# Routing slots by token blocks, one narrowing step fewer in four experts, and a third buffer for f

## The chip, the cores and the metric

The kernel runs on one core of one Trainium2 chip. The metric is the device time of the whole program in microseconds (us); it is given as the median of several runs.

## What is computed

Three parts follow one another. First a linear attention with a decay for each key dimension, over 4 batches, 8 heads, 768 steps and 48 dimensions a head; its output is taken as 3072 tokens of 384 numbers. Then a mixture of eight experts in which every token has one expert and every expert exactly 384 tokens, dealt out greedily by the logits. Last a gated network behind an RMS norm. Cut to what matters:

```python
f = 1 / (1 + exp(-f_logit))                       # attention, for every batch and head
for t in range(768):
    state = f[t][:, None] * state + outer(k[t], v[t])
    y[t] = q[t] @ state
x = y as [3072, 384]
logits = x @ w_gate                               # experts: 8, capacity 384
for idx in argsort(-logits.flatten()):            # best pair of token and expert first
    give the token to the expert if the token is free and the expert not full
out[mask_e] = relu(x[mask_e] @ w1[e]) @ w2[e]
xn = out / rms(out) * rms_g                       # last network, width 1536
result = (silu(xn @ w2_gate) * (xn @ w2_val)) @ w2_out
```

The three weights of the last network come as float64, so the kernel first narrows them to float32 with integer operations.

## The kernel before, in words

**Attention** (`attention`) works on 16 units, each a pair of heads of one batch. A loop over i interleaves the stages of neighbouring units by hand: `scans(i + 1)` on VectorE (two scans over 768 steps, a product with k), `k_back`, `inner`, `sums` and `values` on TensorE, copies on ScalarE, masks and products with q on GpSimd. `decays(i + 2)` on ScalarE turns raw f into decays. `load("kqf", i + 4)` at the end of an iteration (L638) puts the next loads on SyncE's queue, which works in that order. Raw k and raw q have three buffers, raw f has two (`NR`, L363), so the load of f for unit i + 4 goes into the buffer that `decays(i + 2)` has just read. The first load into each buffer takes all 128 rows with their padding; later ones take the 96 rows that change, in two parts (L381, L384).

**Routing** (`Route`) finds eight thresholds in five steps; each step compares on VectorE (`hits`, L75) and counts on TensorE. The last `choose` writes A, a one-hot choice of an expert for every token, with `is_equal` in two halves (L175). A has the layout [128, expert, block], the token's number being 128 times its block (24 of them) plus its partition, so this write goes with a stride. `slots` (L294) then gives every token its place within its expert: a scan on VectorE (`cum`, L309) adds up A along the blocks for each expert, TensorE multiplies with a triangle and with ones and leaves the count of tokens ahead in `pre`; VectorE takes the choice's own (`pos`, L314), adds over the experts (`ps1`, L316), splits the place into a block of 128 and a rest (L318 to L322), multiplies W by the block's flags (L325), compares the rest with 0 to 127 in three calls of `hits`, and 24 matmuls (L334) turn all into the list `idx` of the tokens of each expert. A gather by `idx` then fetches the rows of the first expert.

**Experts**: `expert(e)` runs over eight column blocks j. For each j TensorE makes `h` (9 matmuls of 384 columns; each product is split into high and low parts, hence three matmuls where one would do, L673 to L675), ScalarE writes `hh` (L1146), VectorE the low part `hl` (L1147), and TensorE does `second(e, j - 2)`, 9 matmuls that read `hh` and `hl` of two blocks earlier. `second` for j = 6 and 7 comes behind the loop. `side(e, j)` puts the other work in between:

```python
if j in ((1, 2, 3, 4) if e == 0 else (1, 3, 4, 5) if e < 5 else (1, 3, 5)):
    narrow_step()
if 0 < j < 5:
    piece_split(W1[e + 1, j - 1])        # high and low part of the next expert's weights
...
if j > 4:
    xpose(e + 1, j - 5)                  # transposes of the next expert's rows
...
if j > 5:
    narrow_step()
```

A `narrow_step` is a stage of a small pipeline: it writes back a finished tile (ScalarE's queue), narrows an earlier one (`narrow2`: L1067 on ScalarE, L1068, L1069, L1071 on VectorE, L1072 and L1073 on GpSimd) and loads another (L1058 on SyncE's queue). There are 36 tiles and 40 calls: six in each of the experts 0 to 4, five in experts 5 and 6, none in the last. The order of the instructions on each engine is the order of the program; no planner moves them.

**Last network**: 12 blocks of 256 tokens, bound to the narrowed weights, mostly TensorE.

Of the kernel before, what the change touches and what calls it, by code (L numbers as in the profile page):

```python
# [35 lines left out]

def more_consts(tc, cst, K):
    nc = tc.nc
    edge = K["edge"]
    inc = cst.tile([128, 128], F32, name="inc")  # L40
    K.update(inc=inc, up=cst.tile([128, 128], BF, name="up"))
    nc.gpsimd.tensor_scalar(inc[:, 0:1], edge[:, 0:1], 1.0, 0.0, op0=OP.mult, op1=OP.add)
    nc.gpsimd.tensor_tensor(out=inc[:, 1:], in0=edge[:, 1:], in1=edge[:, :-1], op=OP.subtract)
    ed = cst.tile([128, 128, 4], BF, name="edges")
    nc.gpsimd.tensor_scalar(ed, edge[:, :, None].to_broadcast([128, 128, 4]), 1.0, 0.0, op0=OP.mult, op1=OP.add)
    up0 = cst.tile([128, 128], BF, name="up0")
    nc.gpsimd.memset(up0, -(2.0 ** -7))
    lim = cst.tile([128, 2], F32, name="lim")
    for c, a, b in ((0, 1.0, -1.0), (1, 384.0, -383.5)):
        nc.gpsimd.memset(lim[:, c:c + 1], a)  # L50
        nc.gpsimd.memset(lim[0:1, c:c + 1], b)
    tri = cst.tile([128, 128], BF, name="tri_bf")
    nc.gpsimd.memset(tri, -1.0)
    nc.gpsimd.affine_select(out=tri, in_=tri, pattern=[[-1, 128]], compare_op=OP.is_ge, fill=0.0, base=0,
                            channel_multiplier=1)
    first = cst.tile([128, 8, 24], F32, name="first")
    nc.gpsimd.memset(first, 1.0)
    nc.gpsimd.memset(first[:, :, 0:1], 0.0)
    ids = cst.tile([128, 24], F32, name="ids")
    nc.gpsimd.iota(ids, pattern=[[128, 24]], base=0, channel_multiplier=0, allow_small_or_imprecise_dtypes=True)  # L60
    pid = cst.tile([128, 1], F32, name="pid")
    nc.gpsimd.iota(pid, pattern=[[0, 1]], base=0, channel_multiplier=1, allow_small_or_imprecise_dtypes=True)
    K.update(tri=tri, first=first, ids=ids, pid=pid, ed=ed, up0=up0, lim=lim)

# [16 lines left out]
class Route:  # L81
# [176 lines left out]
    def run(self, n, flag, idx, ident, rows=None, side=None, more=None):  # L258
# [3 lines left out]

        def check(wk, ps, cum):
# [5 lines left out]
            nc.tensor.matmul(ct[:, 0:E], self.K["ones"], cum[:, :, self.NB - 1], start=True, stop=True)  # L269
            nc.tensor.matmul(ct[:, E:], self.K["ones"], bad, start=True, stop=True)  # L270
            if more:
                more()

            def verdict():
                nc.vector.tensor_scalar(c9[:, 0:E], ct[:, 0:E], self.CAP, None, op0=OP.not_equal)
                nc.vector.tensor_scalar(c9[:, E:E + 2], ct[:, E:], 0.0, None, op0=OP.not_equal)
                nc.vector.tensor_reduce(out=flag, in_=c9, axis=AX.X, op=OP.max)

            return verdict

        with self.tc.tile_pool(name="rf_wk", bufs=1) as wk:
# [12 lines left out]
def slots(tc, K, A, ident, idx, check=None):  # L294
# [3 lines left out]
    with tc.tile_pool(name="s_wk", bufs=1) as wk, tc.tile_pool(name="s_ps", bufs=1, space=PSUM) as ps:  # L298
        fl = "p e n -> p (e n)"
# [4 lines left out]
        nc.gpsimd.tensor_tensor(out=W[:, 0, :, 0], in0=A, in1=K["pid"][:, 0:1, None].to_broadcast([128, E, NB]), op=OP.mult)  # L304
        nc.gpsimd.tensor_tensor(out=W[:, 1, :, 0], in0=A, in1=K["ids"][:, None, :].to_broadcast([128, E, NB]), op=OP.mult)
# [7 lines left out]
        pos = wk.tile([128, E, NB], F32, name="pos")  # L313
# [22 lines left out]
        spin(nc, ps.tile([128, 128], F32, name="spin"), ident, 12)  # L336
        nc.vector.tensor_reduce(out=t1[:, :, 0:3], in_=tb.rearrange("p j (e c) -> p e c j", c=3), axis=AX.X, op=OP.add)
# [3 lines left out]

def attention(tc, fT, kT, qT, vL, YT, w_gate, lg, pmin, ident, gcol, rms_g, bank0, extra):

# [18 lines left out]
    one = bank0[:, 0:1]  # L362
    NR = dict(f=2, k=3, q=3)  # L363
    RAW = {(nm, i): cst.tile([128, S], F32, name=f"raw_{nm}{i}") for nm in "fkq" for i in range(NR[nm])}
    NV = 4
# [3 lines left out]
    def raw(nm, i):  # L369
        return RAW[nm, i % NR[nm]]  # L370

    def load(names, i):
        if not 0 <= i < NU:
            return
        for nm in names:
# [3 lines left out]
            src, t = dict(f=fT, k=kT, q=qT)[nm][i], raw(nm, i)  # L379
            if i < NR[nm]:  # L380
                nc.sync.dma_start(t, src)  # L381
                continue
# [8 lines left out]

    mask = cst.tile([128, C], F32, name="mask")
    nc.gpsimd.memset(mask, 1.0)
# [8 lines left out]
    lgp = YP[0][:, 384:432].rearrange("p (n e) -> p n e", e=8)  # L402
    sel = cst.tile([128, 2, 2, 3, 8], F32, name="sel")
    for t in YP:
# [64 lines left out]
    def k_back(i, gs=(0, 1)):  # L469
        if 0 in gs:  # L470
            KN[i] = wk.tile([128, NC, 128], F32, name="kn")
        a, m = (0, NC - 1) if len(gs) == 2 else (3 * gs[0], 3 - gs[0])
# [62 lines left out]
    def logits(b):  # L535

        o = bank()[:, 0:256]
        for k in range(NP):
            for r in range(4):
# [7 lines left out]
                                 start=k == 0, stop=k == NP - 1)  # L547
        LG[b] = wk.tile([128, 256], F32, name="lgT")
        nc.scalar.copy(LG[b], o)
# [23 lines left out]
    for i in range(-1, NU + 2):  # L573
# [59 lines left out]
        if i == NU - 1:  # L633
# [3 lines left out]
            extra["edges"](bank())  # L637
        load("kqf", i + 4)  # L638
        if i == NU + 1:
# [153 lines left out]
def tile_kernel(ctx, tc, q, k, v, f_logit, w_gate, w1, w2, w2_gate, w2_val, w2_out, rms_g, fT, kT, qT, vL, out):  # L793
# [32 lines left out]
    lg = rc.tile([128, NT // 128, E], F32, name="lg")  # L826
    A = rc.tile([128, E, NT // 128], BF, name="A")
    pmin = rc.tile([128, 1], F32, name="pmin")
# [8 lines left out]
    def edges(bank):  # L837
        R[0].start(bank)
        R[0].early(ytp, bank0[:, 8:16])

    def consts(bank):
        K.update(route_consts(tc, rc))
        more_consts(tc, rc, K)

# [4 lines left out]
    ctx.enter_context(tc.manual_schedule())  # L849
    attention(tc, fT, kT, qT, vL, YT, w_gate, lg, pmin, ident, gcol, rms_g, bank0,  # L850
              {-2: consts, 1: lambda bank: turn_inc(tc, K, bank[:, 0:128], ident), "range": prepare,
# [59 lines left out]
    with ExitStack() as st:  # L911
        with tc.tile_pool(name="rw", bufs=9) as rw, tc.tile_pool(name="rwp", bufs=4, space=PSUM) as rwp:
            for i in range(4):
# [25 lines left out]
        with tc.If(rv > 0):  # L939
# [6 lines left out]
            with tc.If(rv2 > 0):  # L946
                slow_attention(tc, q, k, v, f_logit, x_dram, w_gate, lg, lg_dram, ident)
                slow_route(tc, K, lg, A.rearrange("p e n -> p n e"), ident)
                slots(tc, K, A, ident, idx)
# [60 lines left out]
    with ExitStack() as c1:  # L1010
# [310 lines left out]
```

## Time and profile before

| | |
|---|---|
| median of 3 runs | 815.48 us (815.25 to 815.67) |
| the profiled execution's own time | 811.92 us |
| span of the profiled execution | 810.2 us |
| TensorE matmul busy | 786.3 us, 97% |
| VectorE busy | 484.5 us, 60% |
| ScalarE busy | 391.0 us, 48% |
| GpSimd busy | 276.3 us, 34% |

A view by stretches gives, for each stretch of the span, how long each engine was busy. The timeline gives single instructions: start, duration, engine, line, operation, written tile, read tile, shape, and in brackets how long the engine stood idle before it and what ended that. PE is TensorE, PEld its weight load, DVE VectorE, ACT ScalarE, POOL GpSimd, SP SyncE.

### The profile page before, as it was taken

The numbers are of one execution on the slowest core, as the hardware profiler recorded it, in microseconds if no ns is written. First come the engines' busy times: TensorE is split into PE (matmuls) and PEld (weight loads), VectorE is DVE, ScalarE is ACT, GpSimd is POOL, SyncE is SP. The second block draws the span as 40 slices with busy tenths as digits, with TensorE's granted clock in tenths as the row PEclk, the third lists the DMA queues.
The fourth block names the chain that finished last, engine by engine and source line by source line (L and its number), as shares of the span: only waits on it lengthen the run. The fifth ranks groups of instructions, "written<-read, shape, count | busy, mean of one in ns | idle before, by whom it ended". The sixth has DMA issues, their size and how long they took to land.

```text
span 810.2 us, 17022 instructions
## 1 busy us (share of the span) xinstructions
PE 786.3 (97%) x6809; PEld 768.3 (95%) x6809; DVE 484.5 (60%) x854; ACT 391.0 (48%) x853; POOL 276.3 (34%) x332
## 2 busy tenths in 40 slices
PE   8999986999999999999999999999999999999996
PEld 7888875999999899999999999999999999999996
DVE  8999875988988898466344343444443434434331
ACT  5888561564555555665434343434344342424221
POOL 7898603377777776240101111111201011111110
PEclk9999997999999999999999999999999999999999
DMA  8999553787678669231000000000000000000000
GB/s 266 234 235 220 186 180 120 258 305 256 235 259 306 231 244 334 89 113 40 20 1 21 2 20 1 20 2 20 13 8 21 2 20 1 21 1 21 1 20 20
DMA packets 44262, 88.50 MB, mean 109 GB/s; under 512 B 5904, under 2 KB 23568, under 8 KB 44176
## 3 DMA queue, kind: packets, MB, share of 16 engines
q1 hardware_dynamic: 35072, 70.80, 28.1%
q0 software_dynamic: 3104, 9.44, 3.2%
q10 hardware_dynamic: 6000, 7.09, 2.5%
q8 instruction: 55, 0.90, 0.5%
q14 instruction: 31, 0.25, 0.1%
HBM read 70.81 MB, written 16.52 MB: 108 GB/s over the span
## 4 chain that ended last, share of the span: by engine, by line
PE 65%; issue 8%; DVE 7%; DMA 1%; ACT 1%; POOL 1%; POOLq 0%; ACTq 0%; DVEq 0%
PE o L674 5%; PE g L673 5%; PE g L674 5%; PE v L675 5%; PE v L673 5%; PE g L675 5%; PE v L674 5%; PE o L673 5%; PE o L675 5%; PE h L674 3%; PE h L675 3%; PE h L673 3%; PE x L674 3%; PE x L675 2%; PE x L673 2%
## 5 line engine op out<-in xcount | busy, mean ns | idle before, releaser
L1246 DVE TENSOR_TENSOR hf<-sg,v 128x256 f32<-128x256 f32 x144 | 60.0, 416 | 180.4 <-PE v L675 132.1
L1249 ACT CAST hh<-hf 128x256 fp32r<-128x256 f32 x144 | 58.6, 407 | 138.7 <-DVE hf L1246 138.7
L1007 POOL TENSOR_TENSOR xlo<-xn,xhi 128x256 fp32r<-128x256 f32 x36 | 29.5, 823 | 276.1 <-ACT xhi L1006 276.1
L674 PE MATMUL g<-xlo,w 128*128 128x256 f32 x432 | 119.2, 276 | 0.0
L675 PE MATMUL g<-xhi,w 128*128 128x256 f32 x432 | 119.2, 276 | 0.0
L673 PE MATMUL v<-xhi,w 128*128 128x256 f32 x432 | 119.2, 276 | 0.0
L674 PE MATMUL v<-xlo,w 128*128 128x256 f32 x432 | 119.2, 276 | 0.0
L675 PE MATMUL v<-xhi,w 128*128 128x256 f32 x432 | 119.2, 276 | 0.0
L673 PE MATMUL g<-xhi,w 128*128 128x256 f32 x432 | 119.2, 276 | 0.0
L1244 ACT ACTIVATE sg<-g 128x256 f32<-128x256 f32 x144 | 55.4, 384 | 99.4 <-PE g L675 99.0
L1250 DVE TENSOR_TENSOR hl<-hf,hh 128x256 fp32r<-128x256 f32 x144 | 61.3, 425 | 68.1 <-ACT hh L1249 63.3
L674 PE MATMUL o<-w,hh 128*128 128x384 f32 x288 | 97.0, 337 | 0.0
L673 PE MATMUL o<-w,hh 128*128 128x384 f32 x288 | 96.6, 335 | 0.0
L675 PE MATMUL o<-w,hl 128*128 128x384 f32 x288 | 96.2, 334 | 0.0
L673 PEld LDWEIGHTS g<-xhi,w 128*128 128x128 f32 x432 | 81.1, 188 | 0.0
L675 PEld LDWEIGHTS v<-xhi,w 128*128 128x128 f32 x432 | 81.1, 188 | 0.0
L673 PEld LDWEIGHTS v<-xhi,w 128*128 128x128 f32 x432 | 81.1, 188 | 0.0
L674 PEld LDWEIGHTS v<-xlo,w 128*128 128x128 f32 x432 | 81.1, 188 | 0.0
L675 PEld LDWEIGHTS g<-xhi,w 128*128 128x128 f32 x432 | 81.1, 188 | 0.0
L674 PEld LDWEIGHTS g<-xlo,w 128*128 128x128 f32 x432 | 81.0, 188 | 0.0
L870 DVE TENSOR_TENSOR w<-wraw,w 128x1536 fp32r<-128x1536 f32 x35 | 70.7, 2019 | 5.9 <-ACT w L867 5.5
L1072 POOL TENSOR_TENSOR nr<-nr,ne 128x384 f32<-128x384 f32 x36 | 53.1, 1476 | 48.8 <-DVE ne L1071 26.3
(244 smaller groups left out, 1877.4 us busy)
## 6 DMA issues: line engine op xcount, KB each, us to landing
wraw<-in_moe_w_dram SPq DMA_DIRECT2D x32, 768.0 KB, 6.7
v<-in_v_rows_dram SPq DMA_DIRECT2D x16, 288.0 KB, 5.1
x_dram<-xrows SPq DMA_DIRECT2D x24, 192.0 KB, 2.2
nraw<-in_moe_w_gate_dram SPq DMA_DIRECT2D x12, 384.0 KB, 4.2
nraw<-in_moe_w_val_dram SPq DMA_DIRECT2D x12, 384.0 KB, 3.5
nraw<-in_moe_w_out_dram SPq DMA_DIRECT2D x12, 384.0 KB, 3.7
raw_f<-in_f_logit_turned_dram SPq DMA_DIRECT2D x28, 144.0 KB, 4.5
raw_k<-in_k_turned_dram SPq DMA_DIRECT2D x26, 144.0 KB, 5.4
```

Of the source, the lines that this page charges most:

```text
L673: nc.tensor.matmul(out, lhs[0], rhs[0], start=first, stop=False)
L674: nc.tensor.matmul(out, lhs[0], rhs[1], start=False, stop=False)
L675: nc.tensor.matmul(out, lhs[1], rhs[0], start=False, stop=last)
L870: eng.tensor_tensor(out=lo, in0=raw, in1=hi.bitcast(F32), op=OP.subtract)
L1007: eng.tensor_tensor(out=lo, in0=s, in1=hi.bitcast(F32), op=OP.subtract)
L1072: nc.gpsimd.tensor_tensor(out=r, in0=r, in1=e2.bitcast(F32), op=OP.mult)
L1244: nc.scalar.activation(sg, pg, AF.Silu)
L1246: nc.vector.tensor_tensor(out=h, in0=sg, in1=pv, op=OP.mult)
L1249: nc.scalar.copy(hh, h)
L1250: nc.vector.tensor_tensor(out=hl, in0=h, in1=hh.bitcast(F32), op=OP.subtract)
```

## The change

- **A by blocks.** A becomes [128, block, expert]; `choose` writes it without a stride, and everything in `slots` follows that order.
- **Block sums by TensorE.** The scan `cum` and its constant `first` go. Instead two matmuls with A as weights (96 of its columns each) against ones give the sum of each block and expert, laid out with blocks and experts on the partitions; VectorE copies the 96 x 256 result from PSUM to `sums`, and two matmuls of `sums` with a constant `upto` add the blocks up into `pre`. One more matmul stands in `check`. `upto` is made by two GpSimd instructions (`blocks_ahead`) near the end of the attention, from a small constant `of` that VectorE makes at the start.
- **W behind the first comparison.** The two products of W with the flags (old L325) are issued behind the first of the three calls of `hits`.
- **Narrowing.** Expert 0 gets seven steps, experts 1 to 6 five each, the last expert three, of which one narrows a tile and two only write back; 40 in all, as before.
- **Buffers.** Raw f gets three buffers, and the loads of a unit go in the order f, k, q. To make room, `kn` loses its unused last block, `lgT` has one buffer, two small tiles move to another pool, and the pool of `xrows` has 8 buffers in place of 9.

```diff
-    first = cst.tile([128, 8, 24], F32, name="first")
-    nc.gpsimd.memset(first, 1.0)
-    nc.gpsimd.memset(first[:, :, 0:1], 0.0)
+    of = cst.tile([96, 8], F32, name="of")
+    nc.vector.tensor_reduce(out=of, in_=ident[0:96, 0:96].rearrange("k (n e) -> k e n", e=8), axis=AX.X, op=OP.add)
...
+def blocks_ahead(nc, K):
+
+    o = K["upto"]
+    nc.gpsimd.tensor_scalar(o, K["of"][:, None, None, :].to_broadcast([96, 2, 24, 8]), 1.0, 0.0, op0=OP.mult, op1=OP.add)
+    nc.gpsimd.affine_select(out=o, in_=o, pattern=[[-96, 2], [8, 24], [1, 8]], compare_op=OP.is_ge, fill=0.0, base=0,
+                            channel_multiplier=-1)
...
-                m = self.choose(wk, A.rearrange("p e n -> p n e"))
+                m = self.choose(wk, A)
...
-        pre = ps.tile([128, E, NB], F32, name="pre")
+        spare = ps.tile([128, 2, 128], F32, name="spin")
+        for h in range(2):
+            nc.tensor.matmul(spare[0:96, h], A[:, 12 * h:12 * h + 12].rearrange(fl), K["ones"], start=True, stop=True)
+        sums = wk.tile([96, 2, 128], BF, name="sums")
+        nc.vector.tensor_copy(sums, spare[0:96])
+        pre = ps.tile([128, NB, E], F32, name="pre")
         nc.tensor.matmul(pre.rearrange(fl), K["tri"], A.rearrange(fl), start=True, stop=False)
-        cum = wk.tile([128, E, NB], BF, name="cum")
-        nc.vector.tensor_tensor_scan(out=cum.rearrange(fl), data0=K["first"].rearrange(fl), data1=A.rearrange(fl),
-                                     initial=0.0, op0=OP.mult, op1=OP.add)
-        nc.tensor.matmul(pre.rearrange(fl), K["ones"], cum.rearrange(fl), start=False, stop=True)
-        verdict = check(wk, ps, cum) if check else None
+        for h in range(2):
+            nc.tensor.matmul(pre.rearrange(fl), sums[:, h], K["upto"][:, h].rearrange(fl), start=False, stop=h == 1)
+        verdict = check(wk, ps, sums) if check else None
...
-        nc.vector.tensor_reduce(out=ps1, in_=pos.rearrange("p e n -> p n e"), axis=AX.X, op=OP.add)
+        nc.vector.tensor_reduce(out=ps1, in_=pos, axis=AX.X, op=OP.add)
...
-        for c in (1, 2):
-            nc.vector.tensor_tensor(out=W[:, :, :, c], in0=W[:, :, :, 0],
-                                    in1=ge[:, c, None, None, :].to_broadcast([128, 2, E, NB]), op=OP.mult)
...
             hots.update(hits(nc, K["cm"], "ro", K["io"], r, g, 8))
+            for c in (1, 2) if g == 0 else ():
+                nc.vector.tensor_tensor(out=W[:, :, :, c], in0=W[:, :, :, 0],
+                                        in1=ge[:, c, None, None, :].to_broadcast([128, 2, E, NB]), op=OP.mult)
...
-    NR = dict(f=2, k=3, q=3)
+    NR = 3
...
-        load("kqf", i + 4)
+        load("fkq", i + 4)
...
-        with tc.tile_pool(name="rw", bufs=9) as rw, tc.tile_pool(name="rwp", bufs=4, space=PSUM) as rwp:
+        with tc.tile_pool(name="rw", bufs=8) as rw, tc.tile_pool(name="rwp", bufs=4, space=PSUM) as rwp:
...
-                if j in ((1, 2, 3, 4) if e == 0 else (1, 3, 4, 5) if e < 5 else (1, 3, 5)):
+                if j in ((1, 2, 3, 4, 5) if e == 0 else (1, 3, 5)):
                     narrow_step()
...
+                if j in (0, 1, 3):
+                    narrow_step()
                 if j:
                     piece_split(W2[j - 1])
```

## Rows read from the trace of the kernel before

**Rows 1.** Stretches by stage: length, busy us of each engine, granted clock, DMA.

```profile
0.00:104.00 104.00, 100.48 (x1821) 88.90 (x1822) 95.24 (x125) 75.17 (x220) 81.46 (x143) 0.98 0.85 222
104.00:138.00 34.00, 25.27 (x269) 22.23 (x268) 25.31 (x88) 15.11 (x28) 4.62 (x7) 0.85 0.45 158
138.00:357.00 219.00, 214.06 (x1254) 210.96 (x1254) 180.92 (x243) 122.31 (x193) 141.01 (x102) 1.00 0.72 246
357.00:810.00 453.00, 446.52 (x3473) 446.20 (x3471) 183.05 (x401) 178.41 (x413) 49.21 (x81) 1.00 0.04 13
```

**Rows 2.** Waits of TensorE in the experts, 145 to 350 us: total, times, longest.

```profile
PE x L674 <- DVE hl L1147: 4.3, 4, 1.2
```

**Rows 3.** Stretches of 8 us at the ends of experts 4 and 5, same columns.

```profile
269.50:277.50 8.00, 6.59 (x38) 5.95 (x37) 7.68 (x15) 2.73 (x6) 5.34 (x6) 1.00 0.66 224
296.00:304.00 8.00, 8.00 (x50) 7.92 (x49) 7.32 (x13) 3.11 (x7) 4.42 (x5) 1.00 0.69 233
```

**Rows 4.** Timeline of VectorE late in experts 4 and 5, and hl of expert 0.

```profile
164.34 0.55 DVE L1147 SCALAR_TENSOR_TENSOR hl<-h,hh 128x384 fp32r<-128x384 f32 x1
...
270.06 0.71 DVE L1068 TENSOR_SCALAR nb<-nraw 128x384 int32<-128x384 int32 x1
...
272.45 0.55 DVE L1036 TENSOR_TENSOR xlo<-xT,xhi 128x384 fp32r<-128x384 f32 x1
...
275.96 0.55 DVE L1147 SCALAR_TENSOR_TENSOR hl<-h,hh 128x384 fp32r<-128x384 f32 x1
...
295.87 0.70 DVE L1068 TENSOR_SCALAR nb<-nraw 128x384 int32<-128x384 int32 x1
...
297.55 0.55 DVE L1036 TENSOR_TENSOR xlo<-xT,xhi 128x384 fp32r<-128x384 f32 x1
...
301.06 0.55 DVE L1147 SCALAR_TENSOR_TENSOR hl<-h,hh 128x384 fp32r<-128x384 f32 x1
```

**Rows 5.** Timeline of TensorE at the last `second` of experts 0, 4 and 5.

```profile
165.90 0.34 PE L674 MATMUL x<-hl,w 128*128 128x384 f32 x1
...
275.04 0.34 PE L673 MATMUL x<-hh,w 128*128 128x384 f32 x1
276.56 0.44 PE L674 MATMUL x<-hl,w 128*128 128x384 f32 x1 [1.18 <-DVE hl L1147]
...
303.04 0.34 PE L674 MATMUL x<-hl,w 128*128 128x384 f32 x1
```

**Rows 6.** Two lines of the narrowing: ns of one, least, median and most.

```profile
L1069 DVE SCALAR_TENSOR_TENSOR nb<-nraw,nb x36: 557/560/1264, 154.0 to 322.8; 128x384 int32<-128x384 int32 x36
...
L1072 POOL TENSOR_TENSOR nr<-nr,ne x36: 1003/1020/2417, 155.1 to 324.0; 128x384 f32<-128x384 f32 x36
```

**Rows 7.** Timeline of VectorE around the last choice and the slots.

```profile
120.24 0.42 DVE L175 TENSOR_TENSOR oh<-open,m 128x96 bf16<-128x96 f32 x2
...
124.00 0.42 DVE L170 SCALAR_TENSOR_TENSOR open<-T,down 128x96 f32<-128x96 f32 x2 [0.33 <-PE T L242]
124.34 0.40 DVE L173 TENSOR_REDUCE m<-open 128x12 f32<-128x96 f32 x2
124.66 1.02 DVE L175 TENSOR_TENSOR A<-open,m 128x96 bf16<-128x96 f32 x2
...
126.68 0.36 DVE L314 TENSOR_TENSOR pos<-pre,A 128x192 f32<-128x192 f32 x1
127.07 0.62 DVE L316 TENSOR_REDUCE ps<-pos 128x24 f32<-128x192 f32 x1
```

**Rows 8.** Timeline of TensorE in the slots.

```profile
129.53 2.28 PE L334 MATMUL tb<-W,cm 128*128 128x48 bf16 x24 [2.63 <-DVE cm L75]
```

**Rows 9.** Timeline of ScalarE and VectorE at the fourth unit of the attention.

```profile
20.61 0.86 ACT L424 ACTIVATE G<-raw_f 128x768 f32<-128x768 f32 x1 [0.21 <-DMA raw_f<-in_f_logit_turned_dram]
...
21.79 1.75 DVE L450 TENSOR_TENSOR_SCAN P<-G,bank 128x768 f32<-128x768 f32 x1 [0.70 <-ACT fs L427]
```

More of the change, by code (lines that the diff above doesn't have):

```diff
@@ L34, in route_consts, with more_consts @@
     return dict(io=io, ones=ones, edge=bits.bitcast(F32))
-def more_consts(tc, cst, K):
+def more_consts(tc, cst, K, ident):
     nc = tc.nc
@@ L62, in more_consts @@
     nc.gpsimd.iota(pid, pattern=[[0, 1]], base=0, channel_multiplier=1, allow_small_or_imprecise_dtypes=True)
-    K.update(tri=tri, first=first, ids=ids, pid=pid, ed=ed, up0=up0, lim=lim)
+    K.update(tri=tri, of=of, upto=cst.tile([96, 2, 24, 8], BF, name="upto"), ids=ids, pid=pid, ed=ed, up0=up0, lim=lim)
+def blocks_ahead(nc, K):
[3 more added lines that the diff above has]
+                            channel_multiplier=-1)
 def turn_inc(tc, K, bank, ident):
@@ L261, in run, with check @@
         nc, E, A = self.tc.nc, self.E, self.A
-        def check(wk, ps, cum):
+        def check(wk, ps, sums):
             c9, bad = self.c9, self.bad
@@ L268, in check @@
             ct = self.ct
-            nc.tensor.matmul(ct[:, 0:E], self.K["ones"], cum[:, :, self.NB - 1], start=True, stop=True)
+            for h in range(2):
+                nc.tensor.matmul(ct[:, 0:E], sums[:, h], self.K["upto"][:, h, self.NB - 1], start=h == 0, stop=h == 1)
             nc.tensor.matmul(ct[:, E:], self.K["ones"], bad, start=True, stop=True)
@@ L298, in slots @@
     with tc.tile_pool(name="s_wk", bufs=1) as wk, tc.tile_pool(name="s_ps", bufs=1, space=PSUM) as ps:
-        fl = "p e n -> p (e n)"
+        fl = "p n e -> p (n e)"
+        Ae = A.rearrange("p n e -> p e n")
         ge = wk.tile([128, 3, NB], BF, name="ge")
@@ L303, in slots @@
         W = wk.tile([128, 2, E, 3, NB], BF, name="W")
-        nc.gpsimd.tensor_tensor(out=W[:, 0, :, 0], in0=A, in1=K["pid"][:, 0:1, None].to_broadcast([128, E, NB]), op=OP.mult)
-        nc.gpsimd.tensor_tensor(out=W[:, 1, :, 0], in0=A, in1=K["ids"][:, None, :].to_broadcast([128, E, NB]), op=OP.mult)
-        pre = ps.tile([128, E, NB], F32, name="pre")
-        nc.tensor.matmul(pre.rearrange(fl), K["tri"], A.rearrange(fl), start=True, stop=False)
-        cum = wk.tile([128, E, NB], BF, name="cum")
-        nc.vector.tensor_tensor_scan(out=cum.rearrange(fl), data0=K["first"].rearrange(fl), data1=A.rearrange(fl),
-                                     initial=0.0, op0=OP.mult, op1=OP.add)
-        nc.tensor.matmul(pre.rearrange(fl), K["ones"], cum.rearrange(fl), start=False, stop=True)
-        verdict = check(wk, ps, cum) if check else None
-        pos = wk.tile([128, E, NB], F32, name="pos")
+        nc.gpsimd.tensor_tensor(out=W[:, 0, :, 0], in0=Ae, in1=K["pid"][:, 0:1, None].to_broadcast([128, E, NB]), op=OP.mult)
+        nc.gpsimd.tensor_tensor(out=W[:, 1, :, 0], in0=Ae, in1=K["ids"][:, None, :].to_broadcast([128, E, NB]), op=OP.mult)
+        spare = ps.tile([128, 2, 128], F32, name="spin")
[4 more added lines that the diff above has]
+        pre = ps.tile([128, NB, E], F32, name="pre")
+        nc.tensor.matmul(pre.rearrange(fl), K["tri"], A.rearrange(fl), start=True, stop=False)
+        for h in range(2):
+            nc.tensor.matmul(pre.rearrange(fl), sums[:, h], K["upto"][:, h].rearrange(fl), start=False, stop=h == 1)
+        verdict = check(wk, ps, sums) if check else None
+        pos = wk.tile([128, NB, E], F32, name="pos")
         nc.vector.tensor_tensor(out=pos, in0=pre, in1=A, op=OP.mult)
         ps1 = wk.tile([128, NB], F32, name="ps1")
-        nc.vector.tensor_reduce(out=ps1, in_=pos.rearrange("p e n -> p n e"), axis=AX.X, op=OP.add)
+        nc.vector.tensor_reduce(out=ps1, in_=pos, axis=AX.X, op=OP.add)
         for c in (1, 2):
@@ L335, in slots @@
                              start=(n == 0), stop=(n == NB - 1))
-        spin(nc, ps.tile([128, 128], F32, name="spin"), ident, 12)
+        spin(nc, spare[:, 0], ident, 12)
         nc.vector.tensor_reduce(out=t1[:, :, 0:3], in_=tb.rearrange("p j (e c) -> p e c j", c=3), axis=AX.X, op=OP.add)
@@ L339, in slots, with attention @@
         nc.vector.tensor_tensor(out=ix, in0=t1[:, :, 0:3], in1=t1[:, :, 1:4], op=OP.subtract)
-def attention(tc, fT, kT, qT, vL, YT, w_gate, lg, pmin, ident, gcol, rms_g, bank0, extra):
+def attention(tc, side, fT, kT, qT, vL, YT, w_gate, lg, pmin, ident, gcol, rms_g, bank0, extra):
     nc = tc.nc
@@ L362, in attention @@
     one = bank0[:, 0:1]
-    NR = dict(f=2, k=3, q=3)
-    RAW = {(nm, i): cst.tile([128, S], F32, name=f"raw_{nm}{i}") for nm in "fkq" for i in range(NR[nm])}
+    NR = 3
+    RAW = {(nm, i): cst.tile([128, S], F32, name=f"raw_{nm}{i}") for nm in "fkq" for i in range(NR)}
     NV = 4
@@ L369, in raw @@
     def raw(nm, i):
-        return RAW[nm, i % NR[nm]]
+        return RAW[nm, i % NR]
     def load(names, i):
@@ L379, in load @@
             src, t = dict(f=fT, k=kT, q=qT)[nm][i], raw(nm, i)
-            if i < NR[nm]:
+            if i < NR:
                 nc.sync.dma_start(t, src)
@@ L390, in attention @@
     load("fk", 1)
-    mask = cst.tile([128, C], F32, name="mask")
+    mask = side.tile([128, C], F32, name="mask")
     nc.gpsimd.memset(mask, 1.0)
@@ L402, in attention @@
     lgp = YP[0][:, 384:432].rearrange("p (n e) -> p n e", e=8)
-    sel = cst.tile([128, 2, 2, 3, 8], F32, name="sel")
+    sel = side.tile([128, 2, 2, 3, 8], F32, name="sel")
     for t in YP:
@@ L470, in k_back @@
         if 0 in gs:
-            KN[i] = wk.tile([128, NC, 128], F32, name="kn")
+            KN[i] = wk.tile([128, NC - 1, 128], F32, name="kn")
         a, m = (0, NC - 1) if len(gs) == 2 else (3 * gs[0], 3 - gs[0])
@@ L547, in logits @@
                                  start=k == 0, stop=k == NP - 1)
-        LG[b] = wk.tile([128, 256], F32, name="lgT")
+        LG[b] = wk.tile([128, 256], F32, name="lgT", bufs=1)
         nc.scalar.copy(LG[b], o)
@@ L826, in tile_kernel @@
     lg = rc.tile([128, NT // 128, E], F32, name="lg")
-    A = rc.tile([128, E, NT // 128], BF, name="A")
+    A = rc.tile([128, NT // 128, E], BF, name="A")
     pmin = rc.tile([128, 1], F32, name="pmin")
@@ L838, in edges @@
         R[0].start(bank)
+        blocks_ahead(nc, K)
         R[0].early(ytp, bank0[:, 8:16])
@@ L842, in consts @@
         K.update(route_consts(tc, rc))
-        more_consts(tc, rc, K)
+        more_consts(tc, rc, K, ident)
     yt = ExitStack()
@@ L849, in tile_kernel @@
     ctx.enter_context(tc.manual_schedule())
-    attention(tc, fT, kT, qT, vL, YT, w_gate, lg, pmin, ident, gcol, rms_g, bank0,
+    attention(tc, rc, fT, kT, qT, vL, YT, w_gate, lg, pmin, ident, gcol, rms_g, bank0,
               {-2: consts, 1: lambda bank: turn_inc(tc, K, bank[:, 0:128], ident), "range": prepare,
@@ L947, in tile_kernel @@
                 slow_attention(tc, q, k, v, f_logit, x_dram, w_gate, lg, lg_dram, ident)
-                slow_route(tc, K, lg, A.rearrange("p e n -> p n e"), ident)
+                slow_route(tc, K, lg, A, ident)
                 slots(tc, K, A, ident, idx)
```

## The prediction

> **What bounds the kernel now.** I read the stretches by stage first [rows 1]. In the attention (to 104 us) VectorE is busy 95.24 of 104 us: a part of the change helps there only if it shortens VectorE's chain. The routing (104 to 138) is a chain of short steps that hand over between VectorE and TensorE, which is why TensorE shows 25.27 of 34. In the experts (138 to 357) and in the last network TensorE is nearly always busy, 214.06 of 219 and 446.52 of 453, and the only time to be had is the few us in which it stands still. So I asked next what TensorE waits for in the experts [rows 2]: one thing, the low part `hl`, 4 times, 4.3 us in all, 1.2 at most. The stretches show where [rows 3]: at the end of expert 4 TensorE has 6.59 of 8 us and VectorE 7.68, while at the end of expert 5 TensorE is full and VectorE a little freer at 7.32. Expert 4 has six narrowing steps and expert 5 five; the four waits are those of experts 1 to 4, the ones with steps at j = 3, 4 and 5.
>
> The timeline tells how late `hl` is. In expert 4 the last `hl` ends at 275.96 + 0.55 = 276.51 [rows 4]. TensorE began the matmul before at 275.04 and the one that reads `hl` only at 276.56 [rows 5]. Those starts lie 1.52 apart, where neighbours in a full row lie 0.17 apart (an estimate: half of the 0.34 that each shows, as they overlap); so `hl` is needed at about 275.21 and comes 1.30 late, a little more than the 1.18 that the wait shows. In expert 5 `hl` ends at 301.61 and is read at 303.04, 1.43 early.
>
> **The change, part by part.**
>
> *Narrowing.* Experts 1 to 4 lose the step at j = 4. What a step holds VectorE for is read from start to start: 270.06 to 272.45 is 2.39 in expert 4, 295.87 to 297.55 is 1.68 in expert 5 [rows 4]. Without it the last `hl` of expert 4 ends 1.68 to 2.39 earlier and is 0.38 to 1.09 in time: its stall goes, and the other three, none of them longer, go with it. That is worth the 4.3 us of the waits, plus some 0.15 each that the modelled ends hide (1.52 - 0.17 = 1.35 against 1.18): 4.9.
>
> Expert 0 gets a step more, at j = 5, on an engine that has no gap there. Its last `hl` ends at 164.34 + 0.55 = 164.89 [rows 4] and is read at 165.90 [rows 5], 1.01 early. A step of 1.68 to 2.39 makes it 0.67 to 1.38 late: a new stall, of which I take 1.0. Of the step's other work, its load waits behind nothing new on SyncE's queue (the first weight piece of expert 2 is issued two blocks later), its write-back on ScalarE's queue stands after a product finished blocks earlier, and the two GpSimd products come when that engine has only the next narrowing to do; if they come into the way, rival 1 has the price.
>
> Experts 5 and 6 run the pattern that expert 5 has today; expert 6 narrows two tiles more than now, with room as in expert 5 (1.43). The last expert narrows one tile at j = 0 and writes back three. Behind it on VectorE and ScalarE is the first norm's sum of squares, which TensorE reads two blocks on, more than 5 us later by the 18 matmuls a block of 0.17; nothing. The last rows of `w2_out` are so written later, but only the ninth piece of the last network reads them, which waits for the eighth piece's buffer anyway. Sum for the experts: -4.9 + 1.0 = -3.9; bounds -4.9 (no stall in expert 0) to -3.5 (1.38).
>
> *Slots.* The choice without the stride takes what the same line takes for `oh`, 0.42 and not 1.02 [rows 7]: -0.60. The scan goes, and two trips to TensorE with a copy between come. The row for a trip is 0.33, from `ok` to `open` [rows 7], with one matmul; mine have two each, so 0.33 to 0.60 (nothing shows a pair: the upper end doubles the share of the matmul generously). The copy of 256 numbers a partition from PSUM: `pos` reads 192 from there in 0.36, so 0.48, or 0.37 if part of it is fixed. From the end of A to `pos` that is 1.03 to 1.68 against 1.00 now (A ends at 124.66 + 1.02 = 125.68, `pos` starts at 126.68): 0 to 0.7 lost, 0.3 taken, as the row of the trip is the nearest thing. The two small instructions for the verdict run beside the second trip, as they do now beside the matmul. The sum over the experts has its numbers side by side and should take what two halves of such a sum take, 0.40, not 0.62: -0.22, or nothing if the stride is free there. W and the first comparison change places; the first of the 24 matmuls needs both, so its start is not moved, and 2.28 us of them [rows 8] follow as before. GpSimd's first products of W start with A and run ahead of that. Sum: -0.60 + 0.3 - 0.22 = -0.5, bounds +0.1 to -0.8. All of it arrives: gather and first expert follow upon `idx`.
>
> *Buffers.* One wait of VectorE in the attention hangs on f: at the fourth unit 0.70 for `fs`, of which ScalarE itself had waited 0.21 for the load and spent the rest behind its own copies [rows 9]. An f that comes earlier gives back 0.2; at best all of the 0.70. Against it, the third unit's f now comes with its padding rows, 128 rows for 96, a third more to move, and k and q stand behind f: they are issued one load later and used two iterations later. The reduction for `of` falls in VectorE's wait for the first decays; `blocks_ahead` runs on GpSimd after the last mask and before the next thing that engine has to do. Eight buffers for `xrows` hold more than one routing step's five rows. Sum: -0.2, bounds +0.3 to -0.7.
>
> Together -3.9 - 0.5 - 0.2 = -4.6. The sum is made against the profiled execution, 811.92 us (a span of 810.2 with 1.72 around it): 807.3. The runs had a median of 815.48, 3.56 above it; I take the same difference off: **810.9**. What a measurement of this kernel can tell from no change is 0.2%, 1.6 us, so the line runs at 813.85.
>
> **The rivals.** *1. Part of the stalls stays.* The same narrowing instruction takes 0.56 at the median and 1.26 at worst, and its partner on GpSimd 1.02 and 2.42 [rows 6]: the two engines hold each other up, and the new pattern meets in another phase. In expert 4 the margin is 0.38 to 1.09; two instructions of one step's length that each lose 0.7 use it up. If 0.5 us stays in each of experts 1 to 4, the gain is 4.6 - 2.0 = 2.6: 812.9. For it: VectorE is still busy 7.32 of 8 in expert 5. Against it: expert 5 has just this pattern and stands nowhere. The Trainium skill ("SBUF — State Buffer", section "Who interferes with whom") calls this an exclusive lock: a VectorE instruction with two SBUF inputs and a GpSimd one that reads SBUF exclude each other for a whole instruction. The least and the most of these rows agree with that. Going by expert 5 the sum stays 810.9; going by the rule, met once more in each of experts 1 to 4, it is this rival's 812.9.
>
> *2. The stall only moves, and the kernel is slower.* The place is VectorE's queue at j = 5 to 7. If the steps at j = 5, 6 and 7, which stay, were what makes `hl` late, taking j = 4 away would let VectorE only idle earlier; experts 1 to 4 keep 4.9, expert 0 adds 1.4 and expert 6, which gets those steps, 1.3: 815.48 + 2.7 - 0.7 = 817.5. It decides as soon as VectorE has a gap between j = 4 and the last `hl`. Expert 5, which has all three steps and no wait [rows 3], speaks against it.
>
> *3. Only the narrowing pays.* The trips through TensorE take their upper price and the third buffer does nothing or costs 0.3: -3.9 + 0.1 + 0.3 = -3.5, 812.0. For it: TensorE has just stood still when the trips come, and shows 0.85 of its clock over the routing [rows 1]; both trips may run at the lower of its two levels, 1.2 and not 2.4 GHz.
>
> **How the numbers follow.** Forecast 65%, rival 1 18%, rival 2 5%, rival 3 12%. The forecast's own bounds are -4.9 - 0.8 - 0.7 = -6.4 (809.1) and -3.5 + 0.1 + 0.3 = -3.1 (812.4), rarely all at one end; with most of rival 1 the range is 809.6 to 813.6. Rival 1 lies beyond the line in a third of its cases (6%), rival 2 always (5%): faster 0.88, same 0.07 (that 6% and a forecast that falls short for no reason seen), slower 0.05.
>
> **What would show it.** Right: TensorE's waits on `hl` in experts 1 to 4 gone, one of 0.7 to 1.4 us in expert 0; the write of A at 0.42; from the end of A to `pos` 1.0 to 1.7; the sum over experts near 0.40; the wait at the fourth unit's scan shorter by 0.2. Wrong: waits on `hl` in experts 1 to 6, or VectorE with gaps ahead of them; TensorE waiting for the norm in the last expert; `pos` later after A by more than 0.8; a median above 813.6.

## The result and the profile after

The changed kernel took 808.49 us (median of 5 runs, 806.72 to 810.40) where the kernel before took 815.25 in the runs beside it (5 runs, 814.05 to 815.67): a ratio of 0.9916 [0.9895, 0.9937]. Run again later it was 808.38 (6 runs) against 814.08 (11 runs), 0.9935 [0.9915, 0.9956]. It is faster, by 5.7 to 6.8 us, where 4.6 were forecast, and the median of 808.49 lies below the range of 809.6 to 813.6. The profiled execution took 806.72 with a span of 805.0, against 811.92 and 810.2.

The stretches by stage of the changed kernel, and the two of 8 us at the ends of experts 4 and 5 (columns as in [rows 1]):

```profile
0.00:104.00 104.00, 100.00 (x1835) 88.10 (x1836) 97.08 (x130) 76.15 (x222) 83.48 (x143) 1.00 0.84 224
104.00:138.00 34.00, 26.82 (x272) 23.65 (x271) 23.84 (x85) 14.88 (x28) 5.54 (x9) 0.85 0.48 166
138.00:357.00 219.00, 216.46 (x1285) 214.58 (x1284) 172.52 (x244) 125.14 (x198) 139.28 (x100) 1.00 0.70 245
...
269.50:277.50 8.00, 8.00 (x47) 8.00 (x46) 4.44 (x9) 5.33 (x10) 5.74 (x7) 1.00 1.00 355
296.00:304.00 8.00, 8.00 (x47) 8.00 (x46) 3.88 (x8) 5.74 (x10) 5.83 (x6) 1.00 1.02 369
```

In the same 104 us VectorE got through more of its chain (97.08 against 95.24), and TensorE stands still for 2.5 us of the experts where it stood still for 4.9. The 8 us stretches lie at the same times from the start and do not hold the same instructions, as everything now comes earlier; what counts in them is that TensorE is full in both.

What TensorE of the changed kernel waits for in the experts, 145 to 350 us (total, times, longest; [rows 2] answer to it):

```profile
PE xT L995 <- ACT xhi L990: 1.3, 1, 1.3
PE x L686 <- DVE hl L1162: 1.1, 1, 1.1
```

The four waits on `hl` of 4.3 have become one of 1.1, in expert 0, and there is a new one, on `xhi`: the first norm, in the last expert.

VectorE of the changed kernel: the scans of the third and fourth unit, the last choice and the slots, and two adds of the norm ([rows 7, 9]):

```profile
15.23 1.72 DVE L462 TENSOR_TENSOR_SCAN P<-G,bank 128x768 f32<-128x768 f32 x1
20.56 1.72 DVE L462 TENSOR_TENSOR_SCAN P<-G,bank 128x768 f32<-128x768 f32 x1
...
122.55 0.42 DVE L182 TENSOR_TENSOR A<-open,m 128x96 bf16<-128x96 f32 x2
...
123.32 0.42 DVE L319 CAST sums<-spin 96x256 bf16<-96x256 f32 x1 [0.35 <-PE spin L317]
...
124.17 0.36 DVE L326 TENSOR_TENSOR pos<-pre,A 128x192 f32<-128x192 f32 x1
124.56 0.35 DVE L328 TENSOR_REDUCE ps<-pos 128x24 f32<-128x192 f32 x1
...
328.76 2.17 DVE L987 TENSOR_TENSOR nraw<-nraw 128x256 f32<-128x256 f32 x2 [0.40 <-ACT nraw L986]
```

The fourth scan has no wait left. A now starts at 122.55 and not at 124.66, 2.1 earlier: 1.3 of that lies between the starts of the third and the fourth scan (5.33, and 6.60 in the kernel before), the rest behind. 0.56 of the rest is this execution's own: from the last scan of P to the last of `st` it took 8.92, the kernel before 9.48, and the five later traces of the changed kernel and its variants take 9.38 to 9.46. From the start of A to that of `ps` it is 2.01, and was 2.41.

TensorE of the changed kernel: the wait in expert 0, then the last expert's first matmul on `hl` and the norm's two matmuls:

```profile
164.64 0.45 PE L686 MATMUL x<-hl,w 128*128 128x384 f32 x1 [1.11 <-DVE hl L1162]
...
328.53 0.34 PE L686 MATMUL x<-hl,w 128*128 128x384 f32 x1
...
331.43 0.39 PE L995 MATMUL xT<-xhi,onesr 128*128 128x256 f32 x1 [1.32 <-ACT xhi L990]
331.88 0.39 PE L996 MATMUL xT<-xlo,onesr 128*128 128x256 f32 x1
```

The same two instructions in the kernel before:

```profile
335.82 0.34 PE L674 MATMUL x<-hl,w 128*128 128x384 f32 x1
...
337.23 0.28 PE L982 MATMUL xT<-xhi,onesr 128*128 128x256 f32 x1
```

The norm's matmul followed the reader of `hl` by 1.41; now it follows by 2.90. The second matmul then starts 0.45 behind the first instead of 0.12, and counted from the last expert's first matmul on `hl`, its last one comes 1.93 later than it did.

Between the two profiled executions 5.2 us of span went: 2.1 ahead of A, 0.55 from the start of A to that of `idx` (7.43 to 6.88), 2.8 in the experts; the gather and the last network took 0.3 more.

### The profile page after: what moved, and what is told of

The parts are those of the page before. It is cut to its first block, busy times and chain, and to the rows that moved or that the text cites. A ratio compares the mean times of both kernels' runs of the same rounds, so it can differ in the third digit from the quotient of the medians.

```text
span 805.0 us, 17025 instructions
## 1 busy us (share of the span) xinstructions
PE 784.6 (97%) x6813; PEld 767.3 (95%) x6813; DVE 474.7 (59%) x855; ACT 391.0 (49%) x853; POOL 277.4 (34%) x332
## 4 chain that ended last, share of the span: by engine, by line
PE 71%; issue 7%; DVE 2%; DMA 2%; POOL 1%; ACT 1%; POOLq 0%; DVEq 0%; ACTq 0%
PE o L686 5%; PE g L685 5%; PE g L686 5%; PE v L686 5%; PE v L687 5%; PE v L685 5%; PE g L687 5%; PE o L685 5%; PE o L687 5%; PE h L686 4%; PE h L687 4%; PE h L685 4%; PE x L686 3%; PE x L687 3%; PE x L685 3%
## 5 line engine op out<-in xcount | busy, mean ns | idle before, releaser
L883 DVE TENSOR_TENSOR w<-wraw,w 128x1536 fp32r<-128x1536 f32 x35 | 68.4, 1954 | 5.3 <-ACT w L880 4.9
```

Of the source, the lines that this page charges most:

```text
L883: eng.tensor_tensor(out=lo, in0=raw, in1=hi.bitcast(F32), op=OP.subtract)
```

## The experiments

Each part alone first, with the kernel before run again for its own spread.

**e1_narrow**: the kernel before with the new narrowing.

```diff
-                if j in ((1, 2, 3, 4) if e == 0 else (1, 3, 4, 5) if e < 5 else (1, 3, 5)):
+                if j in ((1, 2, 3, 4, 5) if e == 0 else (1, 3, 5)):
...
+                if j in (0, 1, 3):
+                    narrow_step()
```

> Only the narrowing steps are moved, everything else is as before. Theory (the sum with the two stalls that the changed kernel's trace shows): the four waits on hl in experts 1 to 4 go (-4.9 us), expert 0 gets one of about 1.1, and TensorE waits about 1.4 for the norm at the start of the last expert: -2.4 us, ratio about 0.997. Rival (the prediction as it stood, no wait for the norm; the one in the changed kernel came from its other parts): -3.9 us, ratio 0.995, and no wait of TensorE on the cast of the squares' sum.

812.21 us against 814.32, ratio 0.9979 [0.9963, 0.9994]. TensorE's waits in the experts:

```profile
PE xT L982 <- ACT xhi L977: 1.1, 1, 1.1
PE x L674 <- DVE hl L1149: 0.9, 1, 0.9
```

So both the stall in expert 0 and the one at the norm belong to the narrowing. It is worth 0.21%, 1.7 us [0.5, 3.0], not 3.9. The trace of its attention shows something that the edit doesn't touch, the wait ahead of the fourth scan:

```profile
24.76 1.75 DVE L450 TENSOR_TENSOR_SCAN P<-G,bank 128x768 f32<-128x768 f32 x1 [3.01 <-ACT fs L427]
```

**e2_buffers**: the kernel before with three buffers of raw f, the order f, k, q, and the tiles that make room.

```diff
-    NR = dict(f=2, k=3, q=3)
+    NR = 3
...
-        load("kqf", i + 4)
+        load("fkq", i + 4)
```

> Only f's third buffer, the order f, k, q and the room made for it. Theory (the loads at the start really come sooner): TensorE does not wait for v of the first unit, the spins behind it run at the full clock, the fourth unit's scan starts near 20.6 us, and the time falls by 2 us or more, ratio 0.9975 or less. Rival (the early landing of v in the changed kernel's trace was chance): the wait for v is there again, the fourth unit's scan starts between 21 and 22 us, and the time falls by 0.2 us, ratio 0.9995 to 1.

811.11 us, ratio 0.9957 [0.9942, 0.9972]: 3.5 us [2.3, 4.7] where 0.2 was forecast and 0.7 the bound. Its fourth scan starts at 21.08, 5.32 behind the third, with no wait ahead of it. Of the theory's signs, TensorE's wait for `v` of the first unit is gone and the granted clock is 1.00 over the first 40 us; the scan is later than the 20.6 expected and lies where the rival had it. b_again shows why the signs at `v` decide nothing.

**e3_slots**: the kernel before with the choice by blocks, the sums by TensorE and the moved products of W. It has the room for small tiles too, as e2_buffers has.

```diff
-        cum = wk.tile([128, E, NB], BF, name="cum")
...
+        sums = wk.tile([96, 2, 128], BF, name="sums")
+        nc.vector.tensor_copy(sums, spare[0:96])
```

> Only the slots: A by blocks, block sums by TensorE, W behind the first comparison (and the room for small tiles as changed); narrowing and loads as before. Theory: -0.5 to -0.6 us from the start of the write of A to the end of idx, ratio 0.9993. Rival (part of the 2 us that the attention gained comes from the smaller tiles or the missing constants): -2 us or more, ratio 0.9975.

813.52 us, ratio 0.9991 [0.9972, 1.0011]: too small to be timed, as forecast. From A to `idx` its trace has 6.91 us. The three ratios together make 0.9927, which is what the whole change shows (0.9916 and 0.9935): the parts add up. Its fourth scan, with the old order of the loads, and a wait of TensorE for a load of `v` a little earlier:

```profile
24.45 1.76 DVE L462 TENSOR_TENSOR_SCAN P<-G,bank 128x768 f32<-128x768 f32 x1 [2.12 <-ACT fs L439]
```

```profile
20.43 1.04 PE L517 MATMUL U<-v,kn 128*48 128x48 f32 x20 [2.15 <-DMA v<-in_v_rows_dram]
```

Behind that wait the granted clock was 0.50, the lower level, from 20 to 26 us, and VectorE's scan of `st` waited 1.1 for U.

**b_again**: the kernel before, unchanged.

> The kernel before once more, for a second trace. Theory (the wait for v at the start is what this order of loads gives): the wait of TensorE for v of the first unit is there again, 1 us or more, and the clock falls to half behind it. Rival (chance): no such wait in this trace. Ratio 1.000 by both.

813.09 us, ratio 0.9990 [0.9973, 1.0007]. Its fourth scan, and ScalarE at the same unit:

```profile
22.50 1.75 DVE L450 TENSOR_TENSOR_SCAN P<-G,bank 128x768 f32<-128x768 f32 x1 [1.70 <-ACT fs L427]
```

```profile
21.32 0.85 ACT L424 ACTIVATE G<-raw_f 128x768 f32<-128x768 f32 x1 [2.63 <-DMA raw_f<-in_f_logit_turned_dram]
```

Against 0.70 and 0.21 in [rows 9]: the same program waited a different time in each of its two traces, and the one that I read was the milder. The traces with the old order and two buffers show 0.70 (before), 1.23 (e6_whole, below), 1.70 (here), 2.12 (e3_slots) and 3.01 (e1_narrow).

The expectation was about another load on the same queue, `v` of the first unit. TensorE waited 1.43 for it in the kernel before:

```profile
12.69 0.96 PE L505 MATMUL U<-v,kn 128*48 128x48 f32 x20 [1.43 <-DMA v<-in_v_rows_dram]
```

There the granted clock stood at 0.50 from 13 to 16 us. Here the wait is 0.71 and the clock stays at 1.00, which is neither the theory's 1 us or more nor the rival's none: this wait, too, differs from execution to execution.

The second group takes the buffers' part to pieces.

**e4_order**: the kernel before, the loads' order alone.

```diff
-        load("kqf", i + 4)
+        load("fkq", i + 4)
```

> The kernel before with the loads of a unit in the order f, k, q; f keeps two buffers. Theory O (f stood last in the queue, and its place is what counts): ScalarE's wait for f of the fourth unit (0.21 to 4.48 us in the four traces with the old order) goes, TensorE's wait for v of the second unit with it, the scan of the fourth unit starts near 21 us, ratio 0.996 to 0.997. Theory B (the third buffer counts, by the one whole load of the third unit's f that comes with it and lets k and q be issued sooner): the waits stay, ratio 0.999 to 1.000.

811.54 us against 813.67, ratio 0.9980 [0.9961, 0.9999]; theory O had 0.996 to 0.997. Its sign came, the fourth scan with no wait:

```profile
20.85 1.72 DVE L450 TENSOR_TENSOR_SCAN P<-G,bank 128x768 f32<-128x768 f32 x1
```

**e5_third**: the third buffer and the room made for it, with the old order (`NR = 3`, and `load("kqf", i + 4)` as it was).

> f in three buffers with the room made for it, the loads in the old order k, q, f. Theory O: f of the fourth unit is still late, ScalarE waits 1 us or more for it, ratio 0.998 to 1.000. Theory B: no wait there, k of the third unit is issued at 8 to 9 us where it was 10.2 to 11.6, ratio 0.996 to 0.997.

812.07 us, ratio 0.9975 [0.9962, 0.9989]. The wait stays, at the low end:

```profile
22.29 1.75 DVE L450 TENSOR_TENSOR_SCAN P<-G,bank 128x768 f32<-128x768 f32 x1 [0.67 <-ACT fs L427]
```

**e6_whole**: two buffers and the old order, but the third unit's f loaded with its padding rows in one DMA, as the third buffer makes it.

```diff
-            if i < NR[nm]:
+            if i < 3:
```

> The kernel before, but f of the third unit comes in one load of 128 rows where it came in two of 48; two buffers, old order. It gives what of theory B is the number of loads and not the buffer. Theory O: nothing, ratio 0.999 to 1.000. Theory B by the loads: k of the third unit is issued 2 us sooner and the wait for f of the fourth unit shrinks, ratio 0.997; B by the buffer: nothing.

813.40 us, ratio 0.9998 [0.9983, 1.0013], and a wait of 1.23. The whole load alone gives nothing that the runs can tell.

```profile
22.40 1.75 DVE L450 TENSOR_TENSOR_SCAN P<-G,bank 128x768 f32<-128x768 f32 x1 [1.23 <-ACT fs L427]
```

What the order does is seen on SyncE's queue. The kernel before issues f of the fourth unit here (a row of two DMAs, its length that of both):

```profile
14.78 1.82 SPq L384 DMA_DIRECT2D raw_f<-in_f_logit_turned_dram  x2
```

and the changed kernel here:

```profile
11.31 0.81 SPq L396 DMA_DIRECT2D raw_f<-in_f_logit_turned_dram  x2
```

Both halves are out at 12.12 and not at 16.60, with k and q behind them. The order alone has the first of them at 11.73 (e4_order), the third buffer alone at 14.27 (e5_third). The wait is gone in every trace that has the order, eight in all (e2_buffers, e4_order, two of the changed kernel, four of its variants below). How the 3.5 us divide between order and buffer stays open: each alone times at 0.20% and 0.25%, together at 0.43%, with intervals that overlap. The gain of the third buffer alone is clear of zero, which its theory O did not expect (0.998 to 1.000 where 0.9975 came); but its one trace still shows the wait, so what it saved in the runs isn't shown.

The last group takes the changed kernel, to look for the two stalls that the narrowing left.

**after_again**: the changed kernel, unchanged.

> The changed kernel once more, on the chip of the next three. Ratio to the kernel before 0.9916 as measured; its trace is to show again no wait for f at the fourth unit, about 1.1 us on hl in expert 0 and about 1.3 us on the cast of the squares' sum in the last expert.

808.38 us, ratio 0.9935 [0.9915, 0.9956], with the same two waits: 1.1 on `hl` in expert 0, 0.8 on `xhi`.

**e7_norm**: the norm's steps a block later.

```diff
-        NORM0 = {(E - 1, 0): [n0.squares], (E - 1, 2): [n0.total], (E - 1, 3): tail0[0:2], (E - 1, 4): tail0[2:3]}
+        NORM0 = {(E - 1, 1): [n0.squares], (E - 1, 3): [n0.total], (E - 1, 4): tail0[0:3]}
```

> The changed kernel with the first norm started one block later: squares at j = 1, their sum at j = 3, the reciprocals at j = 4 of the last expert. Theory (the narrowing step at j = 0 stands ahead of the squares on ScalarE and waits there for a write-back): TensorE's wait on the cast goes, 1.3 us less than the changed kernel, ratio to it 0.9983. Rival (the norm is late for its own length, and the next wait takes the time back): no gain, and TensorE waits for the scaled xn at the start of the last network.

809.61 us, ratio 0.9945 [0.9924, 0.9966]; the theory failed. The wait on `xhi` is still 0.7, and short ones on `hl` come in the last expert. A block more did not make the norm punctual.

**e8_move**: expert 0's seventh step goes to expert 6.

```diff
-                if j in ((1, 2, 3, 4, 5) if e == 0 else (1, 3, 5)):
+                if j in ((1, 2, 3, 4) if e == 0 else (1, 3, 4, 5) if e == 6 else (1, 3, 5)):
```

> The changed kernel with expert 0's seventh step moved to expert 6 (j = 4): six steps in expert 0, six in expert 6. Theory (margins of the last hl in the changed kernel: 2.2 us in expert 6, a step takes 1.7 to 2.4): the wait of expert 0 goes, expert 6 waits at most 0.2 us, 1.1 us less than the changed kernel, ratio to it 0.9986. Rival (the stall moves along with the step): a wait of about 1 us on hl in expert 6, ratio 1.000.

807.52 us, ratio 0.9927 [0.9904, 0.9951]. The waits of TensorE:

```profile
PE xT L995 <- ACT xhi L990: 1.2, 1, 1.2
PE x L686 <- DVE hl L1162: 0.8, 1, 0.8
```

The second is now in expert 6: the stall moves with the step, and the time can't be told from the changed kernel's. The sixth step, at j = 4, costs expert 6 about 1 us (27.26 against 26.14, table below), as it cost experts 1 to 4 before.

**e9_both**: the edits of e7_norm and e8_move.

> Both edits of the two runs before it. Theory: TensorE stands nowhere in the experts but at their start, 2.3 us less than the changed kernel, ratio to it 0.997, to the kernel before 0.989. Rival: one of the two stalls comes back in another place, ratio to the changed kernel 0.9985 or more.

808.31 us, ratio 0.9932 [0.9908, 0.9956]: 0.3 left on `xhi`, 1.3 on `hl` in three waits. Again no gain over the changed kernel can be told.

**e10_writeback**: the norm's lateness traced to its beginning. ScalarE of the changed kernel late in expert 6 and early in the last one:

```profile
317.13 0.33 ACTq L1094 DMA_DIRECT2D w_o<-nr  x1
...
324.35 0.55 ACT L1080 ACTIVATE nr<-nraw 128x384 f32<-128x384 uint32 x1 [3.27 <-DMA w_o<-nr]
...
327.57 0.55 ACT L1080 ACTIVATE nr<-nraw 128x384 f32<-128x384 uint32 x1 [1.14 <-DMA w_o<-nr]
...
330.97 0.40 ACT L990 CAST xhi<-nraw 128x256 fp32r<-128x256 f32 x1 [1.93 <-DVE nraw L987]
```

The first product of a narrowing stands and waits for its buffer, `nr`, which the write-back of an earlier tile has to free; the steps at j = 6 and 7 of expert 6 and j = 0 of the last follow each other block by block, with three buffers. The edit has GpSimd write the last six tiles back as soon as it has added them.

```diff
-            if len(done) > 1 or (done and not ready):
+            late = len(todo) < 5
+            if len(done) > (0 if late else 1):
                 nc.scalar.dma_start(*done.pop(0))
             if len(ready) > 1 or (ready and not todo):
-                done.append(narrow2(*ready.pop(0)))
+                if late:
+                    nc.gpsimd.dma_start(*narrow2(*ready.pop(0)))
+                else:
+                    done.append(narrow2(*ready.pop(0)))
```

> The changed kernel, with the last six narrowed tiles (those whose products come in expert 6 and at j = 0 of the last expert) written back by GpSimd's queue right behind their own addition, in place of ScalarE's queue two steps later. Theory: the norm is late because ScalarE stands at the first product of the narrowing (3.27 and 1.14 in the changed kernel) for the write-back that frees one of the three buffers of nr; with the write-back some 7 us earlier both stalls go, the squares start about 1 us sooner, TensorE's wait for the norm's cast (1.3) and the 0.4 us of the two norm matmuls behind it go, and the time is 1 to 2 us below the changed kernel's ratio of 0.9935: 0.991 to 0.9925. Rival a: what holds the norm is VectorE's adds beside GpSimd's product (2.17 for two); then ScalarE's stalls go and the wait stays at 0.7 or more, ratio 0.993 to 0.995. Rival b: GpSimd's issue of a write takes time of that engine, hl or the products come later, and the time is the same or worse, 0.9935 to 0.996.

807.70 us against 814.19, ratio 0.9925 [0.9903, 0.9947]. The waits of TensorE, then ScalarE, then TensorE in the last expert:

```profile
PE x L686 <- DVE hl L1166: 0.8, 1, 0.8
PE xT L996 <- DVE xlo L991: 0.3, 1, 0.3
```

```profile
322.89 0.56 ACT L1080 ACTIVATE nr<-nraw 128x384 f32<-128x384 uint32 x1
...
327.67 0.54 ACT L1080 ACTIVATE nr<-nraw 128x384 f32<-128x384 uint32 x1
...
331.22 0.41 ACT L990 CAST xhi<-nraw 128x256 fp32r<-128x256 f32 x1 [1.47 <-DVE nraw L987]
```

```profile
330.45 0.34 PE L686 MATMUL x<-hl,w 128*128 128x384 f32 x1
...
331.86 0.28 PE L995 MATMUL xT<-xhi,onesr 128*128 128x256 f32 x1
```

Both stalls of ScalarE are gone, and the norm's matmul follows the reader of `hl` by 1.41 again, as before the change; 0.3 is left ahead of its second matmul. That the write-back made the norm late is shown in the traces. The time fell where the theory had it, but the interval holds the changed kernel's ratio too, so no version is shown to beat it.

**The experts side by side.** From the starts of TensorE's matmuls on `hl` in the traces: from the first of one expert to the first of the next, and in the last expert from the first to the last (us).

| | 0 | 1 | 2 | 3 | 4 | 5 | 6 | last |
|---|---|---|---|---|---|---|---|---|
| before | 26.14 | 27.19 | 27.82 | 27.70 | 28.13 | 26.37 | 26.42 | 20.02 |
| e1_narrow | 27.29 | 26.14 | 26.14 | 26.14 | 26.14 | 26.14 | 26.14 | 22.03 |
| after | 27.47 | 26.10 | 26.28 | 26.31 | 26.27 | 26.30 | 26.28 | 21.95 |
| after_again | 27.44 | 26.22 | 26.42 | 26.42 | 26.42 | 26.42 | 26.42 | 21.73 |
| e7_norm | 27.34 | 26.37 | 26.42 | 26.42 | 26.42 | 26.42 | 26.42 | 22.73 |
| e8_move | 26.14 | 26.14 | 26.14 | 26.14 | 26.14 | 26.14 | 27.26 | 21.84 |
| e9_both | 26.14 | 26.14 | 26.14 | 26.14 | 26.14 | 26.14 | 27.13 | 22.26 |
| e10_writeback | 27.35 | 26.37 | 26.42 | 26.42 | 26.42 | 26.42 | 26.42 | 20.54 |

The four stalls of before stand out as 1.05 over 26.14 and 1.40, 1.28 and 1.71 over 26.42, 5.4 in all; the new one of expert 0 is 0.9 to 1.4; the last expert pays 1.7 to 2.0 for its narrowing, 2.2 to 2.7 where the norm was moved as well (e7_norm, e9_both), and 0.5 where the write-back is out of the way.

## Why the prediction was right and wrong

**Buffers: the term that failed.** The prediction took -0.2, "at best all of the 0.70". Both figures came from [rows 9], so from one execution. The wait for f is a wait for a transfer at the start of the kernel, and it was 0.70, 1.23, 1.70, 2.12 and 3.01 in the five traces with the old order and two buffers; the eight with the new order have none. From the third scan to the fourth these five take 6.60 to 8.94, those eight 5.32 or 5.33: 1.3 to 3.6 us, against 3.5 [2.3, 4.7] in the runs of e2_buffers. Not all of it is f: in three of the five (before, e1_narrow, e3_slots) VectorE's scan of `st` waited another 0.4 to 1.1 for TensorE's U. From the fourth scan to the last the five take 64.65 to 65.19, the eight 64.20 to 64.53, a little more of the same sign. The mechanism (f earlier, scan earlier) was the right one; its size was bounded by the rows read, when nothing said that the row repeats. The forecast did note that the profiled execution was 3.56 below the median of the runs, and it carried that difference over unchanged. Part of it can have been this wait, which the change removes; that is argued and not shown, as the timed runs have no trace.

**Narrowing: the step "nothing" failed.** The stalls of experts 1 to 4 went as forecast, worth 5.4 in the trace read, for the 4.9 taken. Expert 0's new stall of 1.11 lies in the 0.67 to 1.38 worked out. But the prediction costed the norm in the last expert at nothing, as TensorE reads it "more than 5 us later by the 18 matmuls a block of 0.17". It counted the time to the reader and not what stands ahead of the squares: ScalarE's product of the narrowing, which waited 3.27 and 1.14 for a write-back. The three steps in a row put the wait for a buffer of `nr` onto TensorE's path. For expert 0 the prediction did look at where a write-back is issued (it "stands after a product finished blocks earlier"), but not at when it lands. The rows shown of the kernel before don't have this wait, but its trace does: ScalarE waited for write-backs of `nr` 12 times in the experts, 16.4 us in all, though no wait of TensorE was put down to it.

```profile
ACT nr L1067 <- DMA w_v<-nr: 5.6, 4, 1.9
ACT nr L1067 <- DMA w_g<-nr: 5.5, 4, 2.0
ACT nr L1067 <- DMA w_o<-nr: 5.3, 4, 1.9
```

In the last expert it cost 1.9, of which 0.5 is left in e10_writeback. So -5.44 + 1.15 (e1_narrow, expert 0) + 2.01 (its last expert) = -2.3, against 1.7 [0.5, 3.0] in its runs, in place of -3.9. The list of signs did name it: "TensorE waiting for the norm in the last expert".

**Slots: right.** A takes 0.42 as forecast; from its end (122.97) to `pos` it is 1.20 (1.20 to 1.45 in the seven traces that have the new slots), within 1.03 to 1.68, for a copy of 0.42 and a first trip of 0.35; the sum over experts 0.35 for the forecast 0.40. The stretch from A to `idx` fell by 0.55, and -0.5 was the sum; over all traces it is 6.88 to 7.12 with the new slots and 7.37 to 7.45 with the old. The runs of e3_slots alone can't tell so small a gain from none.

**Together:** two errors of opposite sign, 3.3 too little for the buffers and about 2 too much for the narrowing; the parts as timed make 1.7 + 3.5 + 0.7 = 5.9.

**The rivals.** None came. No wait on `hl` stays in experts 1 to 4, against rivals 1 and 2: VectorE and GpSimd did not hold each other up to the point where it counts. Rival 3 had the buffers at nothing, and they paid most. The rule weighed under rival 1 did bite, though elsewhere: the two adds of the norm took 2.17 together beside GpSimd's product (from 328.50 to 329.51) and addition (from 329.59) in the changed kernel, and 0.42 and 0.43 in the kernel before, where GpSimd ran nothing at that time. That is what the Trainium skill says of two engines that exclude each other ("SBUF — State Buffer", section "Who interferes with whom"). With the write-back out of the way the norm was late by only 0.3 with adds still slowed (1.57 for the two), so it was not what decided.

## What to carry to other kernels

In these runs a wait on a transfer was a draw and not a number: where the profiled execution is faster than the median of the runs, look for such waits first, and bound them by several executions or far wider than the row. When a step is moved next to others like it, count the buffers and the write-backs that free them, and not only the engines: three steps in a row found three buffers too few. A step costed at nothing needs everything ahead of it on its own engines to be looked at, not only the distance to its reader.

## What was not expected of the hardware

- The same program, in the same order, kept ScalarE waiting 0.21 us for the load of f in one execution and 2.63 in another (before, b_again); the queue and the bytes were the same.
- With TensorE never waiting and the granted clock shown as 1.00, an expert takes 26.14 us in some executions, 26.42 in others and about 26.28 in that of the changed kernel (table above), and in the kernel before it goes from the first to the second. The single matmuls show it too: a median of 336 ns in e8_move and 338 in after_again, for the same shape. It is 1.1% of the experts, 2 us, as much as the parts argued about here; e7_norm and after_again ran at 26.42, e1_narrow and e8_move at 26.14, so spans of single traces can't rank them. What sets it stays open.
- A write-back of 192 KB in the experts held its buffer for some 7 us: ScalarE issued it at 317.13 and the product that needed the buffer started at 324.35. The same writes issued by GpSimd in e10_writeback landed after 2.3 us at the median (its page's list of DMA issues: engine, count, size, time to landing); for ScalarE's own twelve to `w_o` the median is 6.5 us in the kernel before and 4.4 in after_again. Why ScalarE's take longer wasn't tried.

```profile
w_o<-nr POOLq DMA_DIRECT2D x6, 192.0 KB, 2.3
```
